# Loading the first tiles of an attention and gated-linear kernel in another order: two column halves for tile 0, x tiles ahead of weight rows, nine dummy matmuls

## The chip, the cores and the metric

The kernel runs on one core of one Trainium2 chip. The metric is the device time of one execution in microseconds (us), lower is better. The engines of the core are PE (TensorE, matmuls), DVE (VectorE), ACT (ScalarE), POOL (GpSimd) and SP (SyncE, which here only issues DMAs).

## The reference

Two blocks read the same normalized input and are added to it. The sequence has 2048 positions, the width is 640, there are 32 heads of 20.

```python
xn = _layernorm(x)                                   # (x - mean) / sqrt(var + 1e-5)
qkv = (xn @ wqkv) -> q, k, v per head                # wqkv: 640 x 1920
idx = pos[:, None] - 2 * arange(8)[None, :]          # 8 keys, every second position back
logits = q . k[idx] * Dh ** -0.5 ; masked where idx < 0
o = softmax(logits) . v[idx]
A = o @ wo                                           # 640 x 640
B = ((xn @ w_gate) * (xn @ w_up)) @ w_down           # 640 -> 1536 -> 640
return x + A + B
```

## The kernel before

The 2048 positions are 16 tiles of 128 (numbered t), or four blocks of 512 (j). The 640 columns are five chunks of 128 (c).

**The front.** For each tile t, `front(t)` lays out a chain. The tile is loaded into a slot of `XST`. DVE takes `bn_stats` of the two column halves (L574, "STATS") and joins them with `bn_aggr` (L577, "MV"). ACT takes the square root (L584, "SD"), DVE the reciprocal (L591), and the normalized tile is written to `XNS` (L603 for tiles 0 and 1, in two column pieces; L606 on DVE for tiles 2 to 5; L609 on ACT from tile 6 on). The tile is then transposed into `XNT`: by PE and a copy out of PSUM for tiles 0 to 3 (L642; copies at L653, L655, L662), by a DMA transpose for the rest (L675). From tile 4 on, two tiles share one square root and one reciprocal. Tile 1's statistics wait in the program for tile 0's normalized tile; the first half of tile 2's waits for tile 1's.

**The projections.** Q and K of tiles 0 and 1 (L730) are computed in two parts: the rows of chunks 0 and 1 of the weights first, those of chunks 2 to 4 after that. So PE can begin when the first chunks of `XNT` and the first weight rows are there. A part is a unit: ten or fifteen matmuls that follow one another. The later tiles use whole groups (L698). Then come V, the sliding products on DVE, the softmax, the weighted sums on DVE and POOL (L1192, L1197), which PE sums in four batches (L1251), and the gate, up and down projections on PE (L1315, L1416, L1467).

**The dummies.** `warm(10, JB)` (L1531, body at L680) puts ten matmuls of 512 columns on a constant into PE's queue before the first tile is there. Three more of 256 columns follow tile 0's transposes.

**The order of the work.** The order of each engine's instructions is not written by hand. A planner (`Sched.run`) walks through tasks with a clock for each engine. For each operation the code gives a duration (`occ`), and for some loads a due time (`land`). On each engine it takes, of the tasks that can begin within the engine's patience of the earliest one, the one with the lowest priority number. The patience is 0.25 us for DVE and 0.1 us for the others. The chip then runs each engine's list in that order, with semaphores where one engine needs another's result. So a changed due time or duration can change the order on every engine, to the end of the kernel.

SP issues the loads in the order in which the code names them: tile 0, three chunks of Q's rows, tile 1, the other two chunks, three chunks of K's rows, tile 2, the other two. The tiles 3 to 11, all of V's rows and the tiles 12 to 15 follow from `loads()`.

Of the kernel before, what the change touches and what calls it, by code (L numbers as in the profile page):

```python
# [11 lines left out]
NCH = 5  # L12
# [9 lines left out]
TS = 128  # L22
JB = 512
HB = 1024
QB = 256
DHALF = D // 2
# [329 lines left out]
def build_kernel(nc, A_x, A_wqkv, A_wo, B_x, B_w_gate, B_w_up, B_w_down, out):  # L356
# [5 lines left out]
    def sb(name, shape, dtype=BF16, at=None):  # L362
        n = mybir.dt.size(dtype)
        for s in shape[1:]:
            n *= s
        n = (n + 63) // 64 * 64
        if at is None:
            at = place[0]
            place[0] += n
        assert at + n <= 229344, (name, at + n)  # L370
        return K.sbuf(name, shape, dtype, at)
# [10 lines left out]
    NXS = 12  # L382
    XST = sb("XST", [128, NXS, D], at=a_ot + NCH * JB * 2)
# [77 lines left out]
    def mark(*k):  # L461
        done.add(k)
# [4 lines left out]
    def have(*k):  # L467
        return lambda: k in done

    def num(n, *k):  # L470
        return lambda: count.get(k, 0) >= n

    xhbm = A_x[0]
    ohbm = out[0]

    def dma(o, i, r=(), w=(), name="", eng="sp", group=None, land=None):
        n = mybir.dt.size(o.dtype)
        for s in o.shape:
            n *= s
        return op(eng, lambda e: e.dma_start(o, i), r=r, w=w, dma=True, name=name, nbytes=n, group=group, land=land)  # L480
# [6 lines left out]
       r=[IDENT[:]], w=[IDENT[:]], name="ident", occ=0.4)  # L487
    op("pool", lambda e: e.memset(SEL[:], 0.0), w=[SEL[:]], name="sel", occ=0.1)
    for q in range(4):
        op("pool", (lambda q: lambda e: e.affine_select(SEL[:], SEL[:], pattern=[[-1, 32]], compare_op=ALU.not_equal, fill=1.0,  # L490
                                                        base=-32 * q, channel_multiplier=1))(q),
           r=[SEL[:]], w=[SEL[:]], name=f"sel{q}", occ=0.2)
# [3 lines left out]
       r=[G[:]], w=[G[:]], name="g1", occ=0.3)  # L496
    op("pool", lambda e: e.affine_select(G[:], G[:], pattern=[[-4, H]], compare_op=ALU.is_ge,
                                         fill=0.0, base=0, channel_multiplier=1),
       r=[G[:]], w=[G[:]], name="g2", occ=0.3)
# [8 lines left out]
    def xslot(t):  # L508
        return t + 4 if t < 8 else t - 8

    def x_load(t, eng="sp", land=None):
        dma(XST[:, xslot(t), :], xhbm[t * TS:(t + 1) * TS, :], w=[XST[:, xslot(t), :]], name=f"xld{t}", eng=eng, land=land)
        mark("x", t)

    wqkv_src = A_wqkv.rearrange("(c p) n -> p c n", p=128)

    def wqkv_load(g, lo=0, hi=NCH, eng="sp", land=None):
        dst = WQKV[:, WPOS[g], lo:hi, :]
        dma(dst, wqkv_src[:, lo:hi, g * D:(g + 1) * D], w=[dst], name=f"ld_wqkv{g}_{lo}", eng=eng, land=land)

    def loads():
        def t(f, *a):
            return Task("sp", lambda: f(*a), prio=0)

        for t_ in range(3, NXS):
            yield t(x_load, t_)
        yield t(wqkv_load, 2)
        for t_ in range(NXS, NT):
            yield have("apply", t_ - NXS)
            yield t(x_load, t_)  # L530

        def w(T, src):
            dma(T[:], src.rearrange("(c p) n -> p c n", p=128), w=[T[:]], name="ld_w")

        def pads():
            z = ZERO[:, 0:PAD].unsqueeze(1).to_broadcast([128, NCH, PAD])
            dma(vscr[:, 0:PAD].rearrange("(c p) s -> p c s", p=128), z, r=[ZERO[:, 0:PAD]], w=[("vscr", "pad")], name="vpad")

        yield have("xnt", NT - 1)
        yield t(w, WG, B_w_gate)  # L540
        yield t(pads)
        yield t(w, WU, B_w_up)

        def copy_x():
            a, b = ohbm[0:3 * JB, :], xhbm[0:3 * JB, :]
            o, i = a.rearrange("(p r) n -> p (r n)", p=128), b.rearrange("(p r) n -> p (r n)", p=128)
            op("sp", lambda e: e.dma_start(o, i), w=[("outx",)], dma=True, name="outx", nbytes=2e6)

        yield num(2, "lg")
        yield t(copy_x)  # L550
# [15 lines left out]
    def front(t):  # L566
        x, st = XST[:, xslot(t), :], STATS[:, t, 0:12]
        xs, mv = XNS[:, t % NXN, :], MV[:, t, 0:2]
        sd, rstd, nmr = SD[:, t, 0:1], SD[:, t, 1:2], SD[:, t, 2:3]
        p = 0.1 * t  # L570

        def stats(i):
            o, a = st[:, 6 * i:6 * i + 6], x[:, i * DHALF:(i + 1) * DHALF]
            op("dve", lambda e: e.bn_stats(o, a), r=[a], w=[("st", t, i)], name=f"bn{t}_{i}", occ=0.49)  # L574
# [4 lines left out]
        ts = next((g for g in GROUPS if t in g), (t,))  # L579
        t0, t1 = ts[0], ts[-1] + 1  # L580

        def sqrt():
            o, i = SD[:, t0:t1, 0:1], MV[:, t0:t1, 1:2]
            op("act", lambda e: e.activation(o, i, ACT.Sqrt, bias=EPSC[:, 0:1]), r=[("mv", k) for k in ts] + [EPSC[:]],  # L584
               w=[("sd", k) for k in ts], name=f"sd{t}", occ=0.25)
            for k in ts:
                mark("sd", k)

# [27 lines left out]
        for i in range(2):  # L616
            if t == 2 and i == 0:
                yield have("apply", 1)
            if t == 2 and i == 1:
                yield have("xnt", t - 1)  # L620
            if t in BN_AFTER and i == 1:
                yield have("rstd", t - 1)
            yield Task("dve", lambda: stats(i), r=[x], prio=p)
        yield Task("dve", aggr, r=[("st", t, 1)], prio=p)
        mark("mv", t)
        if t == ts[-1]:
            yield Task("act", sqrt, r=[("mv", t)], prio=p - 1)
            yield Task("dve", recip, r=[("sd", t)], prio=p)
# [51 lines left out]
    def warm(n, cols=QB):  # L680
        for _ in range(n):
            op("pe", lambda e: e.matmul(PS[:, 7, 0:cols], nc.const_aps.tensor(1.0, (128, 128), BF16), nc.const_aps.tensor(1.0, (128, cols), BF16),
                                        start=True, stop=True), w=[PS[:, 7, :]], name="warm", occ=0.427 if cols > QB else 0.12)
# [834 lines left out]
    H_PRIO = 9  # L1518
    FIN_PRIO = 8

    x_load(0, land=3.2)
    tch = A_wqkv.rearrange("(c k p) n -> k c p n", k=16, c=NCH)[:, :, 0, 0:32]
    stores.append(dma(TCH[0:16], tch, w=[TCH[0:16]], name="touch", eng="act"))
    wqkv_load(0, 0, 3, land=5.3)
    x_load(1, land=5.7)
    wqkv_load(0, 3, NCH, land=7.0)
    wqkv_load(1, 0, 3, land=8.5)
    x_load(2, land=9.0)
    wqkv_load(1, 3, NCH, land=10.0)
    K.t["act"] = 2.1  # L1530
    warm(10, JB)  # L1531

    def misc():
        yield have("xnt", NT - 1)
# [5 lines left out]
        yield Task("act", lambda: op("act", preload, name="exp_preload", occ=1.3), prio=6)  # L1540

    K.spawn(loads())
    for t in range(NT):
        K.spawn(front(t))
# [19 lines left out]
def bass_parallel_sum__sliding_local_dilated__glu_gated_bilinear__prompt_kernel(  # L1564
    nc, A_x, A_wqkv, A_wo, B_x, B_w_gate, B_w_up, B_w_down, out
):
    build_kernel(nc, A_x, A_wqkv, A_wo, B_x, B_w_gate, B_w_up, B_w_down, out)
# [28 lines left out]
```

## Time and profile before

| what | value |
|---|---|
| median of 3 runs | 265.47 us (265.27 to 265.48) |
| the profiled execution | 265.01 us, of which the span of its instructions is 263.3 us |
| PE busy | 258.1 us, 98% of the span |
| DVE, POOL, ACT busy | 218.9, 160.6 and 112.8 us |
| HBM read, written | 25.07 MB, 7.23 MB |

The span runs from the first to the last instruction that the profile keeps; 1.7 us of the execution lie around it. All times inside the profile count from the span's start. "Busy" of PE is modelled from the matmuls' starts, so a busy PE is not always at its peak. A release that is named after "<-" is the last thing that an idle engine waited for.

### The profile page before, as it was taken

The numbers are of one execution on the slowest core, as the hardware profiler recorded it, in microseconds if no ns is written. First come the engines' busy times: TensorE is split into PE (matmuls) and PEld (weight loads), VectorE is DVE, ScalarE is ACT, GpSimd is POOL, SyncE is SP. The second block draws the span as 40 slices with busy tenths as digits, with TensorE's granted clock in tenths as the row PEclk, the third lists the DMA queues.
The fourth block names the chain that finished last, engine by engine and source line by source line (L and its number), as shares of the span: only waits on it lengthen the run. The fifth ranks groups of instructions, "written<-read, shape, count | busy, mean of one in ns | idle before, by whom it ended". The sixth has DMA issues, their size and how long they took to land.

```text
span 263.3 us, 4080 instructions
## 1 busy us (share of the span) xinstructions
PE 258.1 (98%) x1566; PEld 135.9 (52%) x1587; DVE 218.9 (83%) x259; ACT 112.8 (43%) x198; POOL 160.6 (61%) x97
## 2 busy tenths in 40 slices
PE   7999999999999999999999999999999999999996
PEld 3996965444444444444444444444444444445675
DVE  4687899999998798778779999999999989994041
ACT  3559987556612221224258656521350144211300
POOL 3000000000599998899973576799989999999100
PEclk9999999999999999999999999999999999999999
DMA  6964699970479996470249424847779676721621
GB/s 212 373 218 81 121 104 366 416 281 12 122 133 186 217 229 129 88 142 1 62 129 309 88 47 109 169 113 171 177 174 208 149 162 137 110 55 37 94 62 50
DMA packets 47843, 39.78 MB, mean 151 GB/s; under 512 B 23856, under 2 KB 45488, under 8 KB 47792
## 3 DMA queue, kind: packets, MB, share of 16 engines
q1 hardware_dynamic: 44848, 33.29, 49.5%
q0 software_dynamic: 2736, 6.16, 13.6%
q8 instruction: 12, 0.20, 0.3%
q10 hardware_dynamic: 240, 0.07, 0.1%
q14 instruction: 7, 0.06, 0.1%
HBM read 25.07 MB, written 7.23 MB: 123 GB/s over the span
## 4 chain that ended last, share of the span: by engine, by line
PE 91%; ACT 6%; issue 1%; DMA 1%; DVE 1%
PE PS L1315 39%; PE PS L1416 21%; PE PS L698 17%; PE PS L1467 7%; ACT XNS L609 3%; PE PS L730 2%; PE PS L1013 2%; PE PS L1251 2%; DMA XST<-in_A_x_dram 1%; ACT QT L703 1%; PE PS L642 1%; ACT VST L703 1%; ACT KT L703 1%; ACT SD L584 0%; DVE STATS L574 0%
## 5 line engine op out<-in xcount | busy, mean ns | idle before, releaser
L1197 POOL TENSOR_TENSOR SV<-PV 128x1024 bf16<-128x1024 f32 x40 | 94.2, 2522 | 15.7 <-DVE HT L1362 3.6
L1192 DVE TENSOR_TENSOR PV<-VX,PS 128x1024 f32<-128x1024 bf16 (+1 forms) x54 | 90.9, 1729 | 2.3 <-POOL SV L1197 2.3
L698 PE MATMUL PS<-XNT,WQKV 128*128 128x512 bf16 (+2 forms) x384 | 60.0, 316 | 0.5 <-issue 0.3
L1315 PE MATMUL PS<-XNT,WU 128*128 128x512 bf16 x239 | 59.4, 379 | 0.2 <-issue 0.2
L1315 PE MATMUL PS<-XNT,WG 128*128 128x512 bf16 x231 | 57.7, 379 | 0.6 <-ACT LOG L1024 0.2
L698 PEld LDWEIGHTS PS<-XNT,WQKV 128*128 128x128 bf16 x390 | 37.8, 112 | 21.9 <-ACT LOG L1024 0.8
L930 DVE TENSOR_TENSOR PRF<-PS,KT 128x1024 f32<-128x1024 f32 x32 | 37.9, 1217 | 0.3 <-PE PS L698 0.3
L1315 PEld LDWEIGHTS PS<-XNT,WU 128*128 128x128 bf16 x240 | 23.4, 98 | 28.5 <-ACT OT L1260 0.4
L1315 PEld LDWEIGHTS PS<-XNT,WG 128*128 128x128 bf16 x240 | 23.4, 98 | 28.5 <-issue 0.4
L956 POOL TENSOR_TENSOR PRF<-PRF,PRF 128x1024 f32<-128x1024 f32 x8 | 22.0, 2751 | 20.6 <-DVE LOG L1073 20.6
L703 ACT ACTIVATE HT<-PS 128x512 bf16<-128x512 f32 x24 | 14.3, 597 | 34.5 <-PE PS L1315 34.5
L881 DVE TENSOR_TENSOR PRD<-QT,KT 128x2048 bf16<-128x2048 bf16 x24 | 27.3, 1223 | 0.0
L1416 PE MATMUL PS<-HT,WD 128*128 128x512 bf16 x117 | 27.2, 380 | 0.1
L1032 POOL MEMSET LOG<- 32x6 bf16 (+6 forms) x7 | 0.4, 95 | 43.7 <-ACT LOG L1024 43.7
L703 ACT ACTIVATE UX<-PS 128x512 bf16<-128x512 f32 x15 | 9.0, 597 | 40.6 <-PE PS L1416 40.6
L989 POOL TENSOR_TENSOR PRD<-PRF,PRF 128x1024 bf16<-128x1024 f32 x8 | 21.4, 2759 | 0.1
L967 POOL TENSOR_TENSOR PRF<-PRF,PRD 128x1024 f32<-128x1024 f32 x8 | 19.5, 2544 | 0.0
L1416 PEld LDWEIGHTS PS<-HT,WD 128*128 128x128 bf16 x120 | 11.7, 98 | 14.3 <-ACT OT L1260 0.4
L1416 PE MATMUL PS<-OT,WO 128*128 128x512 bf16 x75 | 18.6, 379 | 0.1
L1480 DVE TENSOR_TENSOR FB<-PS,XR 128x320 bf16<-128x320 f32 (+2 forms) x9 | 4.1, 455 | 17.4 <-PE PS L1467 16.9
L1324 DVE TENSOR_TENSOR HT<-HT,PS 128x512 bf16<-128x512 bf16 x18 | 12.3, 684 | 7.0 <-PE PS L1315 7.0
L574 DVE BATCH_NORM_STATS2 STATS<-XST 128x6 f32<-128x320 bf16 x32 | 14.0, 470 | 2.4 <-DMA XST<-in_A_x_dram 2.4
(76 smaller groups left out, 246.4 us busy)
## 6 DMA issues: line engine op xcount, KB each, us to landing
VX<-v_scratch SPq DMA_DIRECT2D x80, 130.0 KB, 3.0
PRF<-PRF POOLq DMA_DIRECT2D x8, 512.0 KB, 5.1
XST<-in_A_x_dram SPq DMA_DIRECT2D x16, 160.0 KB, 5.3
v_scratch<-VST SPq DMA_DIRECT2D x4, 640.0 KB, 6.3
WG<-in_B_w_gate_dram SPq DMA_DIRECT2D x1, 1920.0 KB, 9.8
WU<-in_B_w_up_dram SPq DMA_DIRECT2D x1, 1920.0 KB, 14.0
out_dram<-in_A_x_dram SPq DMA_DIRECT2D x1, 1920.0 KB, 20.0
WD<-in_B_w_down_dram SPq DMA_DIRECT2D x1, 1920.0 KB, 8.1
```

The costliest lines, as they stand in the source:

```text
L698: op("pe", (lambda o, l, x, c, first: lambda e: e.matmul(o, l, x, start=first, stop=(c == NCH - 1)))(o, l, x, c, first), r=[l, x], w=[o], ...
L703: X = op("act", (lambda o, i: lambda e: e.activation(o, i, ACT.Copy))(o, i), r=[i], w=[o], name=name, occ=0.12 + n * 0.9e-3)
L881: op("dve", lambda e: e.tensor_tensor(s[:], qb, kv, ALU.mult), r=[q, rk], w=[s[:]], name=f"prod{j}_{r}_{c}", occ=1.15, lock=True)
L930: X = op("dve", lambda e: e.tensor_tensor(o[:], qb, kv, ALU.mult), r=[q, rk, ("qev", j, c)], w=[o[:]], name=f"prow{j}_{r}_{c}_{q0}", occ=1.17)
L956: yield Task("pool", lambda: op("pool", lambda e: e.tensor_tensor(x, x, y, ALU.add), r=[x, y] + tokens(), w=[x], name=name, occ=2.36, lock ...
L967: yield Task("pool", lambda: op("pool", lambda e: e.tensor_tensor(x, x, z, ALU.add), r=[x, z] + tokens(), w=[x], name=name + "c", occ=2.36 ...
L989: yield Task("pool", lambda: op("pool", lambda e: e.tensor_tensor(o, a, y, ALU.add), r=[a, y] + tokens(), w=[o], name=f"qend{j}_{r}_{q0}", ...
L1192: last[0] = op("dve", lambda e: e.tensor_tensor(p, vw, a, ALU.mult), r=[vv] + rk, w=[p], name=f"pv{u}_{x}_{r0}", occ=0.09 + 1.1 * nr)
L1197: X = op("pool", lambda e: e.tensor_tensor(o, p[:, :, 0, :], p[:, :, 1, :], ALU.add), r=[p[:]] + tokens(), w=[o], name=f"pva{u}_{x}", occ= ...
L1315: op("pe", (lambda l, x, c: lambda e: e.matmul(PS[:, b, :], l, x, start=(c == 0), stop=(c == NCH - 1)))(l, x, c), r=[l, x], w=[PS[:, b, :] ...
L1416: op("pe", (lambda l, x, i: lambda e: e.matmul(PS[:, b, :], l, x, start=(i == 0), stop=(i == n - 1)))(l, x, i), r=[l, x], w=[PS[:, b, :]], ...
L1467: op("pe", (lambda l, x, i: lambda e: e.matmul(dst, l, x, start=(i == 0), stop=(i == n - 1)))(l, x, i), r=[l, x], w=[PS[:, b, :]], name=f" ...
```

## The change

The first tile is loaded as two column halves of 320 columns, and tile 0's first `bn_stats` waits for the first half only. The first Q transfer of three chunks becomes one of one chunk and one of two. Tile 1 goes ahead of chunks 1 and 2 of Q's rows, tile 2 ahead of all of K's rows, tile 3 ahead of K's last two chunks (it was loaded after them). SP therefore issues two more transfers. The due times that the planner is given are changed with them, and so is the duration that it assumes for the square root: 0.36 us in place of 0.25 us. One of the ten dummy matmuls is left out.

```diff
+    def x_half(i, land):
+        c = slice(i * DHALF, (i + 1) * DHALF)
+        dma(XST[:, xslot(0), c], xhbm[0:TS, c], w=[XST[:, xslot(0), c]], name=f"xld0_{i}", land=land)
+        if i:
+            mark("x", 0)
...
-        for t_ in range(3, NXS):
+        for t_ in range(4, NXS):
             yield t(x_load, t_)
...
-               w=[("sd", k) for k in ts], name=f"sd{t}", occ=0.25)
+               w=[("sd", k) for k in ts], name=f"sd{t}", occ=0.36)
...
-            yield Task("dve", lambda: stats(i), r=[x], prio=p)
+            yield Task("dve", lambda: stats(i), r=[x[:, i * DHALF:(i + 1) * DHALF]] if t == 0 else [x], prio=p)
...
-    x_load(0, land=3.2)
+    x_half(0, land=2.8)
+    x_half(1, land=3.25)
     tch = A_wqkv.rearrange("(c k p) n -> k c p n", k=16, c=NCH)[:, :, 0, 0:32]
     stores.append(dma(TCH[0:16], tch, w=[TCH[0:16]], name="touch", eng="act"))
-    wqkv_load(0, 0, 3, land=5.3)
-    x_load(1, land=5.7)
-    wqkv_load(0, 3, NCH, land=7.0)
-    wqkv_load(1, 0, 3, land=8.5)
-    x_load(2, land=9.0)
-    wqkv_load(1, 3, NCH, land=10.0)
+    wqkv_load(0, 0, 1, land=4.0)
+    x_load(1, land=4.5)
+    wqkv_load(0, 1, 3, land=5.4)
+    wqkv_load(0, 3, NCH, land=6.3)
+    x_load(2, land=6.8)
+    wqkv_load(1, 0, 3, land=8.6)
+    x_load(3, land=9.0)
+    wqkv_load(1, 3, NCH, land=9.9)
     K.t["act"] = 2.1
-    warm(10, JB)
+    warm(9, JB)
```

## The prediction

> **What bounds the kernel now.** I read the page first, then a table of windows, to see which engine sets the end and where it rests.
>
> ```profile
> span 263.3 us, 4080 instructions
> PE 258.1 (98%) x1566; PEld 135.9 (52%) x1587; DVE 218.9 (83%) x259; ACT 112.8 (43%) x198; POOL 160.6 (61%) x97
> ```
>
> The windows give for each stretch its length and then the busy time of PE, PEld, DVE, ACT and POOL.
>
> ```profile
> 4.80:5.30 0.50, 0.00 (x2) 0.01 (x1) 0.46 (x3) 0.00 (x0) 0.00 (x0) 1.00 1.10 392
> 5.30:8.20 2.90, 2.86 (x38) 2.22 (x38) 2.33 (x8) 1.13 (x3) 0.00 (x0) 1.00 1.00 336
> 8.20:35.00 26.80, 26.74 (x299) 23.83 (x302) 21.78 (x64) 21.74 (x42) 0.00 (x0) 1.00 0.74 183
> 35.00:120.00 85.00, 84.35 (x446) 40.07 (x452) 77.14 (x80) 35.58 (x61) 49.46 (x35) 1.00 0.75 184
> 120.00:241.00 121.00, 120.16 (x603) 53.91 (x614) 111.59 (x93) 49.67 (x87) 105.25 (x47) 1.00 0.58 130
> ```
>
> From 8.2 to 241 us PE rests 0.06 + 0.65 + 0.84 = 1.55 us in all. So the kernel's end is "when PE's real work begins, plus a fixed amount of work, plus 1.55 us of gaps". An edit of the loads can gain only at the beginning; behind that it can gain at most a part of 1.55 us, but can lose anything by a new gap.
>
> What sets the beginning is in the chain of waits (start, length, what):
>
> ```profile
> 0.82 2.36 DMA XST<-in_A_x_dram
> 3.18 0.02 issue
> 3.20 0.90 DVE STATS L574 x2
> ...
> 4.12 0.22 DVE MV L577
> ...
> 4.37 0.30 ACT SD L584
> ...
> 4.90 0.36 DVE XNS L603
> ...
> 6.26 1.40 PE PS L730 x25
> ...
> 8.21 3.54 PE PS L730 x60
> ```
>
> Tile 0 lands at 3.18, and everything to 5.3 is one strand. The waits show the same, and one wait more that the change touches:
>
> ```profile
> DVE SD L591 <- ACT SD L584: 3.8, 9, 0.7
> DVE STATS L574 <- DMA XST<-in_A_x_dram: 2.4, 2, 2.0
> ```
>
> DVE stood 2.0 us for tile 0 and the rest, 0.45 us, for tile 2 (its statistics begin at 8.61). It stood 3.8 us for nine square roots.
>
> **Tile 0 in halves.** The two statistics take 0.90 us, 0.45 each, and now end at 4.10. A half brings 80 KB in place of 160 KB. At the 390 GB/s that the windows from 4.2 to 5.3 show, that saves 0.21 us of 2.36; at the 209 GB/s of the slice from 2 to 3 us it saves 0.39. So the first half lands 1.97 to 2.15 us after its issue at 0.82, at 2.79 to 2.97. The second is issued in the place of today's second transfer, at 1.27, and lands at 3.24 to 3.42 by the same latencies, at 3.63 if a half takes the whole 2.36 us, and at 3.77 if it takes the 2.5 us of the smallest transfer there (the 5 KB touch on ACT's queue). The end of the statistics is then 2.79 + 0.02 + 0.90 = 3.71 at best, 3.63 + 0.02 + 0.45 = 4.10 without gain, 4.24 at worst. I take 2.93 and 3.38, nearest to the 160 KB row of the same queue: 2.93 + 0.02 + 0.45 = 3.40 for the first, 3.85 for the second. The gain is 0.25 us, between -0.14 and +0.39.
>
> The Trainium skill, in "DMA: Bandwidth & Descriptors", section "Anatomy of one DMA", speaks against this edit: some 2.0 us of a transfer (measured there on GpSimd's path) are fixed, and only the rest grows with the bytes. An estimate by that page puts the second half at 1.27 + 2.0 + 0.19 = 3.46 and the gain at 0.17 us. No row of this trace splits a tile, so it can't be decided here.
>
> **What follows tile 0.** Tile 1 landed at 5.4 (issue at 1.73, 3.7 us), just ahead of its statistics at 5.45, which also had to wait for tile 0's L603 (4.90 to 5.54, overlapping by 0.09). If tile 0 alone were early, tile 1 would be late next. That is why its move counts: it passes two of three chunks of Q's rows, 328 KB, 0.84 us at 390 GB/s, and lands at about 4.6, against a need at 5.45 - 0.25 = 5.20. So the whole strand moves: tile 0's transposes, Q of tile 0 and tile 1's strand. Q of tile 1, now at 8.21, begins at 7.96.
>
> **What the moved loads pass.** Chunks 1 and 2 of Q's rows fall behind 164 KB, 0.42 us: from 5.0 (1.27 + 3.7) to 5.4, needed by the second half of the first part at 6.26 - 0.25 + 5 x 0.056 = 6.3. The last two chunks have the same bytes ahead of them as before and land at 6.25, needed at 6.01 + 15 x 0.056 = 6.85. K's first rows move from 8.1 to 8.5, needed at 7.96 + 25 x 0.059 = 9.4 (60 matmuls took 3.54 us). K's last rows move from 9.5 to 9.9, needed ten matmuls later at 10.0: a cover of 0.1 us only. But the due time 9.9 lies behind the planner's end of K's first part, so by its rule it lays K of tile 1's first ten and tile 2's five transposes ahead of them; the need then is about 10.8. If it didn't, the cost would be some 0.1 us. Two more issues of about 0.48 us stand in SP's queue; V's rows are issued at 9.8 in place of 8.82. They landed at 16.8 because 8 us of bytes were queued, not because of the issue, and PE takes them at 18.76. Cost: nothing.
>
> **Tile 2 early.** Its 0.45 us on DVE vanish, and K of tile 1 no longer has to hide it. PE didn't wait for it (0.06 us of rest from 8.2 to 35), so this is worth nothing by itself. A danger lies in DVE's order: tile 2's first statistics (0.45 us) can now begin with tile 1's copy (L653), which PE waits for. The copy has the lower priority number (-0.9 against 0.2) and both can begin at once, so it stays ahead.
>
> **The square root at 0.36.** At 0.25 it was equal to DVE's patience, so DVE waited for each reciprocal. At 0.36 it takes a later tile's statistics instead, where one has landed. That turns part of the 3.8 us into work, and can put a reciprocal up to 0.45 us later. I followed the rule by hand to tile 5. Tile 3's reciprocal stands behind two statistics; its normalized tile is ready about 13.6, and PE, 0.25 us earlier, gets there at 13.98 - 0.25 = 13.73. A cover of 0.1 us. From tile 4 on the normalized tiles run ahead. Worth nothing, since PE sets the end.
>
> **Nine dummies.** PE rested from 4.80 to 5.30. One dummy less (0.43 us apart by the weight loads) lies in that rest. Worth nothing, unless the clock comes later (below).
>
> **The sum.** 265.01 - 0.25 = 264.76 us for the profiled execution. The median of the runs stood 0.46 above it, so the forecast is 265.2 us, with its own range 264.9 to 265.6. That is 0.1%, and within 0.2% (0.53 us), about what a measurement of this kernel can tell from no change.
>
> **Rivals.**
>
> *Nothing comes of the halves*: the second lands at 3.63 or later, or one of the thin covers fails (K's rows, tile 3: 0.1 us each). 265.3 to 265.6. For it speaks the transfer at 1.27, whose 480 KB took 3.7 us; against it, that its bytes are three times tile 0's.
>
> *More than the halves*: they land at 2.79 and 3.24 (0.39), and the new order drops some of the 1.55 us of gaps; a sixth of them makes 0.25 us. 265.47 - 0.64 = 264.8, faster. Against it: each of these gaps belongs to a change of work on PE that stays (0.16 to 0.18 us in the chain at 47.00, 58.04, 195.53).
>
> *Slower, by the order behind 35 us*: the order is planned anew to the end, and POOL's sums may come late for PE. The place is the third batch:
>
> ```profile
> 218.80 2.36 POOL L1197 TENSOR_TENSOR SV<-PV 128x1024 bf16<-128x1024 f32 x1 [0.15 <-DVE PV L1192]
> 221.47 0.77 PEld L1251 LDWEIGHTS PS<-SV,SEL 128*32 128x32 bf16 x20 [0.42 <-ACT XNT L703]
> ```
>
> POOL ends at 221.16, 0.31 us ahead of PE. If one DVE product of 1.73 us (L1192) comes ahead of POOL's last addition, PE waits 1.73 - 0.31 = 1.42 us, and the time is 265.47 - 0.25 + 1.42 = 266.6. It eats the gain from a slip of 0.56 us on, and shows as slower from 1.1 us on. For it: PE has next to no rest now, so a new order has only room to be worse. Against it: all shifts by a quarter of a microsecond or so, in the same direction.
>
> *The clock*: PE's matmuls begin 0.427 us apart and the granted clock rises at about 4.5 us, as the ninth dummy ends. If it rises late, the 35 matmuls of 128 columns and three of 256 between 5.30 and 8.21 (2.3 us) take up to twice as long: up to 267.5. The Trainium skill, "TensorE: Matmul & The Clock Gate", part 1, says that the clock rises after a window of some 3.4 us of work that doesn't start with the kernel. The rest that follows stays about 0.5 us long, since the transposes come earlier too.
>
> **How the numbers follow.** Forecast 0.40 (of it 0.06 under 264.94), nothing comes of it 0.12, more than the halves 0.24, late sums or a like gap 0.20, the clock 0.04. Faster by over 0.2%: 0.06 + 0.24 = 0.30. Slower: 0.20 + 0.04 = 0.24, and 0.02 of the failed covers, 0.26. The rest, 0.44, is within 0.2%. The range goes from 264.6 to 266.7: it takes in the middle of all but the clock.
>
> **What would show it.** Statistics of tile 0 at 2.95 and ending by 3.85; tile 1's beginning near 5.20; Q of tile 1 near 7.96; PE's rest from 8.2 to 35 still under 0.1 us; in the windows from 35 to 241 about 1.5 us of rest. The forecast is wrong if the second statistics wait past 3.65, if PE rests at K's rows or before tile 3's transposes, or if the rest behind 35 us differs by over half a microsecond.

## The result: slower by 0.7%, and the profile after

| | before | after |
|---|---|---|
| median (us) | 265.47 (265.12 to 266.11, 6 runs) | 267.16 (266.63 to 267.97, 6 runs) |
| profiled execution, its span (us) | 265.01, 263.3 | 267.5, 265.7 |

The ratio is 1.0068, with a 95% interval from 1.0053 to 1.0084. That is 1.7 us slower. The forecast was 265.2 us, and its range ended at 266.7. In the changed kernel the lines that this text names behind the new helper have numbers larger by 6: L730 is now L736, L1315 is L1321, L1324 is L1330.

The page of the changed kernel, and then the table of windows over the same stretches (length, then busy time of PE, PEld, DVE, ACT, POOL, then clock, DMA share and GB/s):

```profile
span 265.7 us, 4102 instructions
PE 260.1 (98%) x1586; PEld 136.2 (51%) x1586; DVE 218.6 (82%) x259; ACT 112.8 (42%) x198; POOL 160.7 (60%) x97
```

```profile
4.80:5.30 0.50, 0.40 (x4) 0.19 (x4) 0.50 (x3) 0.00 (x0) 0.00 (x0) 1.00 0.86 277
5.30:8.20 2.90, 1.91 (x22) 1.53 (x21) 1.70 (x6) 1.16 (x3) 0.00 (x0) 1.00 0.90 272
8.20:35.00 26.80, 26.14 (x301) 23.02 (x302) 21.30 (x65) 20.44 (x39) 0.00 (x0) 1.00 0.73 194
35.00:120.00 85.00, 85.00 (x461) 40.98 (x460) 76.36 (x78) 36.76 (x62) 48.66 (x34) 1.00 0.75 186
120.00:241.00 121.00, 120.36 (x612) 53.59 (x610) 111.94 (x93) 49.69 (x87) 104.65 (x47) 1.00 0.58 130
```

PE now rests 0.99 us between 5.30 and 8.20, where it had rested 0.04, then 0.66 us from 8.2 to 35 and 0.64 from 120 to 241. The waits of PE and DVE name two new causes (us in total, times, longest):

```profile
PE PS L736 <- DMA WQKV<-in_A_wqkv_dram: 1.3, 1, 1.3
...
PE PS L1321 <- DVE XNT L1330: 0.6, 1, 0.6
...
DVE SD L597 <- ACT SD L590: 3.2, 6, 1.0
...
DVE STATS L580 <- DMA XST<-in_A_x_dram: 1.6, 1, 1.6
```

The two DVE lines are what the change was made for: the first tile is waited for 0.3 us less (1.63 in place of 1.97 us), and six square roots are waited for in place of nine. The timeline of DVE shows tile 0's statistics in one piece, beginning at 2.87 (3.20 before), so both halves were there in time:

```profile
2.87 0.89 DVE L580 BATCH_NORM_STATS2 STATS<-XST 128x6 f32<-128x320 bf16 x2 [1.63 <-DMA XST<-in_A_x_dram]
```

The two PE lines are where the time went. The first is in the chain of waits (start, length, what):

```profile
2.67 0.43 SPq L480
3.10 0.04 issue
3.15 5.45 DMA WQKV<-in_A_wqkv_dram
8.60 0.05 issue
8.64 0.75 PE PS L736 x10
9.40 0.13 PE PS L648 x2
9.52 0.02 issue
9.55 0.30 DVE XNT L659
9.85 0.04 issue
9.89 2.71 PE PS L736 x45
```

The chain no longer begins with tile 0. It goes through SP's issues to the last Q rows, which took 5.45 us from issue to landing and arrived at 8.60. Q of tile 1 begins at 9.89, 1.68 us later than before.

The second is at the first batch of sums, near 171 us. PE's timeline and DVE's there, after:

```profile
170.92 1.26 PE L1257 MATMUL PS<-SV,SEL 128*32 128x512 bf16 x20
172.82 0.39 PE L1321 MATMUL PS<-XNT,WG 128*128 128x512 bf16 x1 [0.64 <-DVE XNT L1330]
```

```profile
170.96 1.21 DVE L1198 TENSOR_TENSOR PV<-VX,PS 128x1024 f32<-128x1024 bf16 x1
172.09 0.68 DVE L1330 TENSOR_TENSOR XNT<-XNT,PS 128x512 bf16<-128x512 bf16 x1
```

And PE's there in the kernel before:

```profile
169.23 1.26 PE L1251 MATMUL PS<-SV,SEL 128*32 128x512 bf16 x20
170.43 2.76 PE L1416 MATMUL PS<-HT,WD 128*128 128x512 bf16 x12
```

Before, the down projection (L1416, with WD) followed the sums. In the new order a gate group follows. Its PSUM bank is freed by a DVE multiplication (L1330) that stands behind a product of 1.21 us, so PE stands for 0.64 us. In the profiled executions 1.68 + 0.64 = 2.32 us of the difference of 2.49 are accounted for. That difference is larger than the 1.7 us of the medians: the profiled execution of the kernel before, 265.01 us, is quicker than every other run of it on record (265.06 and more).

### The profile page after: what moved, and what is told of

It reads as the page before. It is cut to its first block, busy times and chain, and to the rows that moved or that the text cites. A ratio compares the mean times of both kernels' runs of the same rounds, so it can differ in the third digit from the quotient of the medians.

```text
span 265.7 us, 4102 instructions
## 1 busy us (share of the span) xinstructions
PE 260.1 (98%) x1586; PEld 136.2 (51%) x1586; DVE 218.6 (82%) x259; ACT 112.8 (42%) x198; POOL 160.7 (60%) x97
## 4 chain that ended last, share of the span: by engine, by line
PE 92%; DVE 2%; DMA 2%; POOL 1%; issue 1%; SPq 1%; ACT 0%
PE PS L1321 36%; PE PS L704 23%; PE PS L1422 21%; PE PS L1473 7%; PE PS L1019 2%; DMA WQKV<-in_A_wqkv_dram 2%; PE PS L736 2%; PE PS L1257 1%; DVE PV L1198 1%; POOL SV L1203 1%; SPq L480 1%; DVE XNT L1330 1%; DVE XNT L1368 0%; PE PS L648 0%; ACT ZERO L709 0%
## 5 line engine op out<-in xcount | busy, mean ns | idle before, releaser
L704 PE MATMUL PS<-XNT,WQKV 128*128 128x512 bf16 (+2 forms) x390 | 60.7, 316 | 0.0
L1321 PE MATMUL PS<-XNT,WG 128*128 128x512 bf16 x240 | 59.7, 379 | 0.6 <-DVE XNT L1330 0.6
L1321 PE MATMUL PS<-XNT,WU 128*128 128x512 bf16 x240 | 59.6, 379 | 0.0
L1321 PEld LDWEIGHTS PS<-XNT,WG 128*128 128x128 bf16 x240 | 23.2, 98 | 29.5 <-DVE XNT L1330 1.6
L1321 PEld LDWEIGHTS PS<-XNT,WU 128*128 128x128 bf16 x240 | 23.5, 98 | 28.3
L962 POOL TENSOR_TENSOR PRF<-PRF,PRF 128x1024 f32<-128x1024 f32 x8 | 20.5, 2570 | 20.5 <-DVE LOG L1079 20.5
L1422 PE MATMUL PS<-HT,WD 128*128 128x512 bf16 x120 | 27.5, 379 | 0.0
L995 POOL TENSOR_TENSOR PRD<-PRF,PRF 128x1024 bf16<-128x1024 f32 x8 | 20.4, 2583 | 0.1
L1422 PEld LDWEIGHTS PS<-HT,WD 128*128 128x128 bf16 x120 | 11.7, 98 | 14.4 <-ACT OT L1266 0.4
L1422 PE MATMUL PS<-OT,WO 128*128 128x512 bf16 x75 | 18.6, 379 | 0.0
L1330 DVE TENSOR_TENSOR HT<-HT,PS 128x512 bf16<-128x512 bf16 x18 | 12.3, 686 | 7.4 <-PE PS L1321 7.3
```

What stands on the lines that cost most here:

```text
L704: op("pe", (lambda o, l, x, c, first: lambda e: e.matmul(o, l, x, start=first, stop=(c == NCH - 1)))(o, l, x, c, first), r=[l, x], w=[o], ...
L962: yield Task("pool", lambda: op("pool", lambda e: e.tensor_tensor(x, x, y, ALU.add), r=[x, y] + tokens(), w=[x], name=name, occ=2.36, lock ...
L995: yield Task("pool", lambda: op("pool", lambda e: e.tensor_tensor(o, a, y, ALU.add), r=[a, y] + tokens(), w=[o], name=f"qend{j}_{r}_{q0}", ...
L1321: op("pe", (lambda l, x, c: lambda e: e.matmul(PS[:, b, :], l, x, start=(c == 0), stop=(c == NCH - 1)))(l, x, c), r=[l, x], w=[PS[:, b, :] ...
L1422: op("pe", (lambda l, x, i: lambda e: e.matmul(PS[:, b, :], l, x, start=(i == 0), stop=(i == n - 1)))(l, x, i), r=[l, x], w=[PS[:, b, :]], ...
```

## The experiments

One theory was that the new order of work did it, another that the loads did it. Within the loads it could be the number of transfers that SP issues ahead of the weights, their size or rows, or the sequence itself. The table has what each kernel gave. "Q1" is the start of Q of tile 1 in the profiled execution. "Later waits" are PE's named waits after Q1, from 0.5 us in total on (smaller ones, 0.2 us, stay in the rest). "Rest" is the profiled time less Q1 and less those waits.

| kernel | median (range), us | ratio [95%] | Q1 | later waits | rest |
|---|---|---|---|---|---|
| before | 265.28 to 265.47 by chip | | 8.21 | | 256.80 |
| after | 267.16 | 1.0068 [1.0053, 1.0084] | 9.89 | 0.64 bank | 256.97 |
| e1 new order, loads of before | 266.34 (266.15–267.66) | 1.0046 [1.0031, 1.0060] | 8.48 | 0.90 bank | 256.97 |
| e2 order of before, new loads | 266.61 (265.98–266.76) | 1.0039 [1.0028, 1.0051] | 9.58 | | 257.03 |
| e3 halves only | 266.06 (265.99–266.92) | 1.0036 [1.0023, 1.0049] | 9.24 | | 256.82 |
| e4 sequence only, tile 0 whole | 265.83 (265.39–266.36) | 1.0018 [1.0009, 1.0027] | 8.40 | 0.8 K's rows | 257.16 |
| e5 tile 0 split by rows | 266.52 (266.28–267.34) | 1.0049 [1.0037, 1.0061] | 9.48 | | 256.86 |
| e6 second half from ACT | 265.38 (265.15–266.23) | 1.0003 [0.9995, 1.0012] | 8.85 | | 256.80 |
| e7 e1, first bank wait mended | 266.31 (266.23–266.52) | 1.0037 [1.0025, 1.0049] | 8.65 | 0.69 bank | 256.91 |
| e8 e7 and e6 | 266.21 (266.08–266.37) | 1.0033 [1.0021, 1.0045] | 8.53 | 0.7 bank | 256.85 |
| e9 e1, both mended | 265.35 (265.14–265.73) | 1.0001 [0.9992, 1.0009] | 8.35 | | 257.03 |
| e10 the changed kernel again | 267.65 (one run) | | 10.02 | 0.6 bank | 257.03 |
| e11 e9 and e6 | 265.59 (265.33–265.92) | 1.0008 [0.9999, 1.0016] | 8.93 | | 256.80 |
| e12 before, half and tile 1 from ACT | 265.12 (264.90–265.94) | 0.9993 [0.9984, 1.0003] | 8.41 | | 256.84 |
| e13 new loads, mended order, x from ACT | 265.16 (264.85–265.74) | 0.9992 [0.9983, 1.0001] | 8.90 | | 256.84 |
| e14 a touch more, and SP waits | 267.62 (267.38–268.68) | 1.0097 [1.0080, 1.0114] | 10.78 | | 256.80 |
| e15 new loads, mended order | 266.23 (266.07–266.57) | 1.0035 [1.0023, 1.0047] | 9.71 | | 256.86 |
| e16 one 5-KB transfer more | 266.14 (265.93–266.21) | 1.0027 [1.0016, 1.0039] | 9.39 | | 256.82 |
| e17 two 5-KB transfers more | 266.44 (266.28–266.62) | 1.0041 [1.0028, 1.0054] | 9.29 | | 257.02 |

The last column is nearly constant: 256.8 to 257.03 in all but e4. So each profiled time is explained by two things that can be read off, when Q1 begins and what PE waits for behind it. A single Q1 says less than a median: with the same loads it was 8.21, 8.35, 8.48 and 8.65 in the kernel before, e9, e1 and e7. Costs below are taken from the medians.

**The two halves of the change, e1 and e2.** e1 has the changed kernel's list of operations on every engine, nine dummies and all, but the transfers of before. e2 has the lists of before and the transfers of the changed kernel.

```diff
 # e1: the due times and the 0.36 us of the change, transfers as before
+    x_load(0, land=2.8)
+    wqkv_load(0, 0, 3, land=5.4)
+    x_load(1, land=4.5)
...
 # e2: the transfers of the change, with due times that keep the order
+    x_half(0, land=3.2)
+    x_half(1, land=3.2)
+    wqkv_load(0, 0, 1, land=5.3)
+    x_load(1, land=5.7)
+    wqkv_load(0, 1, 3, land=5.3)
...
```

> The order of every compute engine is that of the changed kernel, operation by operation; only the transfers are those of the kernel before (tile 0 whole, three chunks of Q's rows, tile 1, ...). Theory L (the loads: in the changed kernel's profile Q's last rows land at 8.60 us and PE rests 1.3 us for them): Q of tile 1 begins near 8.2 us again, no wait of PE for weights, and the time falls to 265.5 to 266.2, of which what is above 265.5 is the new order's (PE's rest of 0.64 us near 172 us). Theory P (the new order costs it all, the late landing is the profiled run's only): 267.0 to 267.3.

> The order of every compute engine is that of the kernel before, operation by operation, with its ten dummies and its 0.25 us for the square root; only the transfers and their order are those of the changed kernel, two halves of tile 0 among them. Theory L: Q's last rows land past 8 us, Q of tile 1 begins at 9 to 10 us, and the time is 266.5 to 267.5. Theory P: the strand of tile 0 gains its 0.3 us and the time is 265.1 to 265.3.

The order alone costs 1.00 us (266.34 against 265.34, a little above the 265.5 to 266.2 expected), the loads alone 1.27 us. Both theories hold, each for its part. The sum, 2.27, is a little more than was measured for both; e2's five runs fall into two groups, near 266.0 and from 266.61 to 266.76. e1's timeline of PE has the bank wait with the early Q1 of 8.48, so it isn't a consequence of late loads:

```profile
171.99 1.03 PE L1321 MATMUL PS<-XNT,WG 128*128 128x512 bf16 x4 [0.90 <-DVE XNT L1330]
```

**The order: e7, e8, e9.** More products of the last block take both factors from ACT's copies, so that ACT frees the bank instead of DVE's multiplication.

```diff
-    FAST = ... + [(3, m) for m in range(4)]
+    FAST = ... + [(3, m) for m in range(6)]   # e7; range(7) in e9
```

> The changed kernel's order of PE with the transfers of the kernel before, and with two more products of the last block (4 and 5) taken from a copy that ACT makes, so that the PSUM bank that PE needs after the first batch of sums is freed by ACT, not by DVE. If PE's wait near 172 us (0.90 us in the run without this edit) is the new order's cost, it is gone and the time is 265.3 to 265.7; if the wait only moves on, it stays at 266.2 to 266.5.

> As the run before it, and tile 0 in two column halves with the second on ACT's queue. If both costs are understood, PE doesn't wait near 172 us, tile 0's statistics end near 3.8, the stream is as before, and the time is 265.0 to 265.3, a gain of 0.1 to 0.4 us on the kernel before. If the halves harm the stream from ACT's queue too: 265.8 to 266.4.

> The changed kernel's order with the transfers of the kernel before, and products 4 to 6 of the last block taken from ACT's copy; on PE only one group of five matmuls (the gate projection of product 11) moves behind a group of the third block's output. In the run with products 4 and 5 the wait of 0.9 us near 172 us was gone and one of 0.7 us stood near 221 us, where that group waited for a bank that DVE frees. If these two waits are the new order's whole cost, neither is there now and the time is 265.3 to 265.7. If the cost lies elsewhere, it stays at 266.1 to 266.5.

In e7 the wait only moved on. The one at 172 went, but the order planned anew had the same kind of wait at the third batch:

```profile
219.75 1.26 PE L1257 MATMUL PS<-SV,SEL 128*32 128x512 bf16 x20
221.71 1.25 PE L1321 MATMUL PS<-XNT,WG 128*128 128x512 bf16 x5 [0.69 <-DVE XNT L1330]
```

e8 has it too, and so missed its 265.0 to 265.3. In e9 that gate group stands behind the down projection (L1422, with WD), no such wait is left, and the time is that of the kernel before:

```profile
219.67 1.26 PE L1257 MATMUL PS<-SV,SEL 128*32 128x512 bf16 x20
220.87 1.90 PE L1422 MATMUL PS<-HX,WD 128*128 128x512 bf16 x8
```

So without the bank waits nothing is left of the order's cost, within e9's interval (0.2 us either way). e9 also has the 0.36 us for the square root, the order that goes with an early tile 2 and nine dummies: together they cost and bring nothing that can be measured.

**The loads, one piece at a time: e3, e4, e5.**

```diff
 # e3: before, and
-    x_load(0, land=3.2)
+    x_half(0, land=3.2)
+    x_half(1, land=3.2)
 # e4: before with tile 0 whole, and the rest of the new sequence
 # e5: before, and tile 0 as two transfers of 64 rows
+        q = slice(64 * i, 64 * (i + 1))
+        dma(XST[q, xslot(0), :], xhbm[64 * i:64 * (i + 1), :], ...)
```

> The kernel before with one edit: tile 0 in two column halves, the first statistics waiting for the first half only; the order of all else as before. If splitting the tile by itself does no harm, the statistics of tile 0 end 0.3 us earlier (3.8) and the time is 265.1 to 265.3. If the small first transfers are what leaves the queues short, Q's rows land late here too: Q's last rows past 7 us and 265.8 to 267.

> The kernel before with the changed order of transfers (one chunk of Q's rows, tile 1, two chunks, two chunks, tile 2, K's first rows, tile 3, K's last rows), but tile 0 whole; the order of compute as before. If the finer Q transfers and the early tiles make Q's last rows late, they land past 8 us and the time is 266.5 to 267.5, as with the halves. If the halves are needed for it, Q's last rows land by 6.5 and the time is 265.3 to 265.6.

> The kernel before with tile 0 loaded in two transfers of 64 rows of 1280 bytes, not of 128 rows of 640 bytes; the order of compute as before. Both statistics wait for both transfers. Theory N (one more small transfer in SP's queue ahead of the weights delays the whole stream, whatever its rows): tile 1 lands near 6.4 as with the column halves, its statistics wait for it, and without the early first statistics the time is 266.0 to 266.5. Theory R (rows of 640 bytes are what costs): tile 1 lands near 5.4 to 5.9 and the time is 265.3 to 265.8.

The halves cost 0.7 us by themselves. In e3 tile 0's strand is early, but tile 1 is late (chain of waits):

```profile
2.21 4.25 DMA XST<-in_A_x_dram
6.45 0.02 issue
6.48 0.90 DVE STATS L580 x2
```

It is issued at 2.21 in place of 1.73 and lands at 6.45 in place of 5.4. Split by rows instead of columns (e5), tile 0 costs 1.2 us (SP's first issues took some 0.6 us each there, in place of 0.4, and tile 0 itself landed at 3.8, not 3.18): what the two have in common is one more transfer. e4 makes one more issue as well, but behind the first Q rows and tile 1; it costs 0.5 us, at K's rows, which is neither of the two outcomes expected.

**Another engine issues: e6, e11, e12, e13.** ACT's queue issues the second half, and in e12 and e13 tile 1 too.

```diff
 # e6 (e11: the same in e9)
+    x_half(0, land=3.2)
+    x_half(1, land=3.2, eng="act")
 # e12 (before) and e13 (new loads, FAST as in e9): also
+    x_load(1, eng="act", ...)
```

> The kernel before with tile 0 in two column halves, the second issued from ACT's queue ahead of the touch; SP's queue holds one transfer for tile 0, as before. Theory N: Q's first rows go out at 1.27 again, tile 1 lands near 5.4, the strand of tile 0 gains 0.3 us and the time is 265.0 to 265.2. Theory R: the stream is late as with both halves on SP, 265.8 to 266.2.

> The first of these four with tile 0 in two column halves, the second from ACT's queue. With both waits of the order gone and the stream as before: 265.1 to 265.5; it gains on the run without the halves only as far as tile 1 doesn't come later than tile 0's strand.

> The order of compute of the kernel before; tile 0's second half and all of tile 1 are issued from ACT's queue, so that SP's queue holds one transfer less ahead of the later weights than before. If SP's issues, 0.45 us each, set when the stream runs, the stream is 0.2 to 0.4 us earlier than before, tile 1 lands by 5.0, Q of tile 1 begins near 8.2 or earlier and the time is 264.8 to 265.2. If the DMA queues themselves are the limit, tile 1 lands near 5.4 and the time is 265.3 to 265.6.

> The changed sequence of loads and the changed order of compute with its two waits taken away; tile 0's second half and tile 1 are issued from ACT's queue, so that SP's queue holds two transfers less ahead of the weights. Theory I (what makes the stream late is the number of SP's issues ahead of the large transfers): 2000 KB are there by about 9.4 us, Q's last rows land by 7, PE doesn't wait for them, Q of tile 1 begins by 8.4 and the time is 264.9 to 265.4. Theory S (the sequence, with its small transfers, does the harm on the DMA queues): 2000 KB past 9.8, PE waits for weights, 266.0 to 266.7.

The same halves cost nothing that can be measured when SP doesn't issue the second one: e6 is 0.7 us faster than e3. They don't bring the 0.3 us expected either: in e6's profiled execution tile 1 landed at 6.05, not at 5.4, and its statistics waited. e11 came out just above its range. e12's time lies in its range, but not for the reason given: tile 1 landed at 5.6, not by 5.0. e13 has the changed sequence, with transfers of the same sizes, and its median shows no cost. SP's queue in e13 (start, length):

```profile
0.82 0.40 SPq L480 DMA_DIRECT2D XST<-in_A_x_dram  x1
1.28 1.40 SPq L480 DMA_DIRECT2D WQKV<-in_A_wqkv_dram  x3
```

All Q rows are issued by 2.7 us; in the changed kernel the last are issued from 3.15 on. So the 0.95 us that the same loads and order cost in e15 (below) go when two issues are taken from SP. That doesn't clear the sequence: e13's profiled execution, the slowest of its eleven, has this in its chain of waits:

```profile
2.21 5.40 DMA WQKV<-in_A_wqkv_dram
...
7.65 0.75 PE PS L736 x10
```

Q's last rows were under way as long as in the changed kernel (5.45 us; 4.0 in the kernel before), only they went out 0.94 us earlier. And what ACT issues also goes through another DMA queue (q10 carried 0.15 MB in e6, 0.07 MB in the kernel before), so these runs don't separate the time of SP's issues from what happens inside SP's queue. e12 and e13 are the only versions with a median more than 0.1 us below the kernel before. Their intervals reach 1.0003 and 1.0001, so a gain isn't shown.

**An issue without bytes: e14, e16, e17.** A copy of the 5-KB touch is issued by SP between tile 0 and Q's first rows.

```diff
     stores.append(dma(TCH[0:16], ..., name="touch", eng="act"))
+    stores.append(dma(TCH[32:48], ..., name="touch2", land=3.2))   # e14: TCH[16:32]
+    stores.append(dma(TCH[64:80], ..., name="touch3", land=3.2))   # e17 alone
```

> The kernel before, order of compute and all, with one more transfer of 5 KB (into a corner that nothing reads) between tile 0 and Q's rows in SP's queue. Theory I: the weights and tile 1 land 0.45 us later, tile 1 near 5.9, and the time is 265.7 to 265.9; if a transfer costs as much again on the DMA side, tile 1 lands past 6.2 and the time is 266.0 to 266.4. If only bytes count, nothing changes: 265.3 to 265.5.

> The kernel before, its order of work unchanged, with one more transfer of 5 KB issued by SP between tile 0 and the first Q rows; nothing waits for it. It moves next to no bytes and leaves tile 0 whole, so it has only the issue of a half of tile 0. Theory I (what counts is the number of issues that SP makes ahead of the weights): the weights are issued some 0.45 us later, Q of tile 1 begins some 0.5 to 1.0 us later than in the kernel before, as with the halves and with the split by rows, 265.8 to 266.5 us. Theory B (what counts is how many packets or bytes are queued): as the kernel before, 265.3 to 265.5 us.

> As e16, with two such transfers of 5 KB, as many extra issues ahead of Q's last rows as the changed kernel has. Theory I: twice the delay of e16, 266.2 to 267.0 us. Theory B: 265.3 to 265.6 us. If the two together cost less than 0.3 us, the delay of the issues alone is hidden, and it is the small transfers with bytes in them that keep the stream slow.

e14 didn't measure what it was made for: SP waited until 3.32 for the first touch and issued Q's rows at 3.70. It shows what a delay of all weights by 2.4 us costs, 2.3 us. e16 has no such wait. It moves next to nothing and costs 0.84 us, about as much as e3 (0.72); two such issues (e17) cost 1.14, so the second adds 0.30 us and not, as expected, the same again. In e16, SP's queue and the windows from 2 to 5 us:

```profile
1.28 0.41 SPq L480 DMA_DIRECT2D TCH<-in_A_wqkv_dram  x1
1.73 0.43 SPq L480 DMA_DIRECT2D WQKV<-in_A_wqkv_dram  x1
```

```profile
2.00:3.00 1.00, 1.00 (x4) 0.35 (x3) 0.00 (x0) 0.54 (x1) 0.59 (x4) 1.00 0.75 161
3.00:4.00 1.00, 1.00 (x5) 0.43 (x4) 0.74 (x2) 0.00 (x0) 0.63 (x5) 1.00 0.69 105
4.00:5.00 1.00, 0.47 (x3) 0.00 (x0) 0.57 (x4) 0.29 (x1) 0.00 (x0) 1.00 0.98 346
```

Q's first rows are issued at 1.73, and the rate is 105 GB/s from 3 to 4 us, where the kernel before has 300. In slices of 0.2 us the rate rises past 250 GB/s, once tile 0 is in, some 2 us after the first weights are issued in all three: at 3.2 in the kernel before (issued at 1.27), at 3.8 in e16 (1.73), at 4.2 in e17 (2.20). Until then little moves, though the DMA engines are shown as 0.69 busy in e16 from 3 to 4 us. So a delay of the issue is a delay of the weights. That isn't the whole of it: Q's first rows landed at 6.2 in e16 and at 6.1 in e17, against 5.0, though they were issued 0.46 us late in the one and 0.93 us late in the other. The runs don't show why the first extra issue costs more than its own time.

**Both again: e10 and e15.** e10 is the changed kernel, run again; e15 is the changed kernel with `FAST` as in e9.

> The changed kernel again, for a second look at where its loads land. If the late landing is the transfers' doing, the stream is late as in the first look (Q's last rows past 7.5 us, PE waits for them, Q of tile 1 at 9 us or later) and the wait of 0.6 to 0.9 us near 172 us is there too; if it was a mishap of that execution, Q's last rows land by 6.7 and Q of tile 1 begins by 8.4. Time 266.6 to 268.

> The changed kernel with its own loads; only the two waits of its order are taken away (products 4 to 6 of the last block from ACT's copy). The loads' share alone: with Q's last rows late and Q of tile 1 near 9.5 to 10 us, 266.3 to 266.8. If the two shares don't add up because the bank waits hide behind the late loads, it is 266.8 to 267.2.

e15 costs 0.95 us against before (266.23 against 265.28): the loads' part, without the order's. With e1's 1.00 this makes 1.95, against the 1.7 measured (1.4 to 2.2 by its interval). e10, a single run, has the same two losses.

One thing stays open, and it is the larger part. In the kernels with the changed loads on SP the stream is slower from 4 to 8 us too, when enough was queued. The windows of the changed kernel and of the kernel before:

```profile
4.00:5.00 1.00, 0.90 (x4) 0.04 (x2) 0.60 (x3) 0.30 (x1) 0.00 (x0) 1.00 0.94 211
5.00:6.00 1.00, 1.00 (x8) 0.77 (x9) 0.99 (x3) 0.60 (x2) 0.00 (x0) 1.00 0.88 287
7.00:8.00 1.00, 0.36 (x7) 0.20 (x4) 0.43 (x2) 0.00 (x0) 0.00 (x0) 1.00 0.77 220
```

```profile
4.00:5.00 1.00, 0.80 (x3) 0.10 (x1) 0.57 (x4) 0.30 (x1) 0.00 (x0) 1.00 1.06 388
5.00:6.00 1.00, 0.70 (x8) 0.50 (x8) 1.00 (x4) 0.38 (x2) 0.00 (x0) 1.00 1.05 316
7.00:8.00 1.00, 1.00 (x17) 0.79 (x14) 0.87 (x4) 0.00 (x0) 0.00 (x0) 1.00 1.05 374
```

From 4 to 5 us the DMA engines are busy for 0.94 of the time and move 211 GB/s, against 1.06 and 388: a byte takes 1.6 times as much of their time (0.94 / 211 against 1.06 / 388). e2, e10 and e15 move 215 to 288 GB/s in that slice. With e16's and e17's extra issues the stream is back at 346 and 294 there and at 393 and 394 in the next, so these explain a delay, not a slow stream. The means over the two stretches say the same (GB/s):

| kernel | 2 to 4 us | 4 to 8 us |
|---|---|---|
| before | 254 | 351 |
| after; e2, e10, e15 | 233; 197 to 203 | 256; 264 to 273 |
| e3, e4 | 148, 233 | 336, 323 |
| e13 | 273 | 329 |
| e16, e17 | 133, 100 | 346, 334 |

The extra issue alone takes bytes from the first stretch. The changed kernel lacks 0.04 MB there and 0.38 MB in the second. Halves and sequence each slow the second stretch little; together, on SP, they slow it by a quarter. What does this wasn't found.

## Why the prediction was wrong, point by point

**The frame held.** "When PE's real work begins, plus a fixed amount of work" is the rest column of the table. What I read as "1.55 us of gaps" behind 8.2 us was in good part something else. The groups of the gate projection, before and after:

```profile
L1315 PE MATMUL PS<-XNT,WG 128*128 128x512 bf16 x231 | 57.7, 379 | 0.6 <-ACT LOG L1024 0.2
```

```profile
L1321 PE MATMUL PS<-XNT,WG 128*128 128x512 bf16 x240 | 59.7, 379 | 0.6 <-DVE XNT L1330 0.6
```

The two kernels do the same 240 matmuls there; the record of before lacks nine of them, and 21 of PE's in all (1566 matmuls beside 1587 weight loads). Where a record is missing, PE seems to rest. In the changed kernel's record PE rests 0.64 us from 9.9 to 241, all of it in the one wait. So the rival "more than the halves" hoped for gaps that were at least partly not there.

**Tile 0 in halves: right in size, not safe.** I took landings at 2.93 and 3.38 and a gain of 0.25 us. In the changed kernel's profile the statistics ran without a break from 2.87 to 3.76, a gain of about 0.33. In e3 it was 0.26. In e2, e10 and e15, with the changed loads too, the second statistics began at 3.86 to 3.94, a loss of some 0.3 us (end near 4.4 in place of 4.10); that is the "worst" end of my bounds, and a little beyond. The rule that I cited from the Trainium skill ("DMA: Bandwidth & Descriptors", section "Anatomy of one DMA": some 2.0 us fixed) put the second half, as an estimate, at 3.46. The measured landings lie on both sides of that.

**What the moved loads pass: the first step that failed.** "The last two chunks have the same bytes ahead of them as before and land at 6.25", with the need at 6.85. The bytes were the same; they landed at 8.60, 2.35 us later. Of this 0.90 us is the issue. Each transfer that SP issues takes it about 0.45 us, so with two more ahead of them Q's last rows were issued at 3.15 in place of 2.25. I priced this as "two more issues of about 0.48 us stand in SP's queue" for V's rows alone and called it nothing, though the same issues stand ahead of every weight row. The other 1.45 us is the transfer itself, 5.45 us in place of 4.0. I used the 390 GB/s of a slice of the kernel before, and the changed kernel moved 256 from 4 to 8 us; why, stays open. Chunks 1 and 2 of Q's rows landed at 6.6, not at 5.4. The cost was 0.95 (e15) to 1.27 us (e2).

The Trainium skill says in "DMA: Bandwidth & Descriptors", section "Issuing engines are not separate DMA queues", that transfers issued by several engines share the same 16 DMA engines, and that issuing from several engines only saves the sequencer's time, usually small beside the transfer. Here the weights went out 0.46 us earlier in e6 than in e3, and the kernel was 0.7 us faster: at this place the saving was not small. The runs don't show that saved issue time is all of it.

**Tile 1 early** was right: predicted at 4.6, issued at 2.20 and landed 2.5 us later, at 4.7. It gained nothing, since Q's last rows came later.

**K's rows: wrong as well, and hidden.** I had them at 8.5 and 9.9. In the changed kernel they were issued at 4.17 and 5.17 and landed 6.3 and 6.7 us later, at 10.5 and 11.9. PE came 1.7 us late itself and didn't wait for them. In e4, where Q of tile 1 begins at 8.40, PE waited 0.8 us for K's rows. That these covers held was luck.

**The square root, tile 2, the dummies: right.** e9 shows no cost of them.

**The clock: not settled by the granted clock.** I read a rise at about 4.5 us. The windows show 1.00 for the kernel before from 0.8 us on, while its dummies still start 0.43 us apart, so that column can't show it. By PE's own times the slow pace lasted longer in the changed kernel: tile 0's five transposes and the three dummies behind them took 0.79 and 0.63 us, in place of 0.63 and 0.50. The wait for Q's last rows hid these 0.3 us. e3, with ten dummies, has 0.75 and 0.85, so the ninth isn't shown to be the cause.

**"All shifts by a quarter of a microsecond or so, in the same direction": the second step that failed.** This was my argument against the rival "slower, by the order behind 35 us", which got 0.20. The planner did shift, and on PE one gate group came ahead of the down projection, behind the sums of the first batch. I looked for the danger where POOL's sums come close to PE, at the third batch, and priced 1.42 us. It came at the first batch, through a PSUM bank that DVE holds, for 0.64 to 0.90 us. The kind of loss was named; its place and its mechanism weren't.

**The range** held one loss at a time. Each alone, about 1.0 us above the kernel before, would have stayed within it at some 266.4; the two came together.

## What to carry to other kernels

At the start of a kernel count the transfers that one engine issues ahead of the first bytes that the matmuls need, and don't price an issue at nothing: one more cost 0.7 to 1.2 us here, for 0.4 to 0.6 us of issue and however few bytes it had, and a second one 0.3 us. Try another engine's queue for the extra ones: ACT issued the same half at no cost that could be measured. Don't carry the rate of one slice over to another sequence of transfers. Where a planner orders the whole program, a changed estimate at the front can put a group behind a buffer that comes free late, far from the edit: compare the two orders at every place where an engine has no slack, and don't take a missing record for a rest.

## What was not expected of the hardware

A DMA of 5 KB that nobody waits for cost 0.84 us of the kernel's time, though SP spent only 0.41 us on it. A second one added only 0.30 us. The second 80-KB half of the same tile landed 1.9 us after its issue in one execution and 2.6 us in three others. And DMA engines that are shown as 0.94 busy moved 211 GB/s in one kernel, where 1.06 went with 388 GB/s in another.
